# Norm outputs in chunks of 96 columns with ones behind each: column sums out of the diagonal matmuls

## The chip, the core and the metric

One core of a Trainium2 chip runs the whole program. The metric is device time in microseconds (us) of one execution. The engines are named as in the profile: PE (TensorE), DVE (VectorE), ACT (ScalarE), POOL (GpSimd) and SP (SyncE, which here only issues DMAs; POOL issues DMAs too). Every engine works through its own instructions in a fixed order and waits where an operand or a buffer is not ready.

## What is computed

A forward and backward pass of a block with two layer norms, a spectral filter and a bilinear gated unit, for 2048 rows of 576 columns (x is 1 x 2048 x 576, F is 4608). Cut to what matters here:

```
h = layernorm(x) * (1 + ca) + sa          # ca, sa, ... : rows of 576, made from c and w_mod
x1 = x + ga * spectral(h)
h2 = layernorm(x1) * (1 + cb) + sb
out = x1 + gb * ((h2 @ w_gate) * (h2 @ w_up)) @ w_down
# outputs: out and the gradients of x, both filter parts, w_gate, w_up, w_down, c and w_mod
```

The gradient of a shift (sa, sb) is the plain sum over all rows of the gradient `gh` that arrives at `h`. That of a scale (ca, cb) is the sum over rows of `gh` times the norm's output `n`, and that of `ga` the sum over rows of `gx` times `y`. These five column sums over 2048 rows (and a sixth, for gb, made elsewhere) are what the change is about.

## The kernel before, in words

The rows are held as 16 row tiles t (128 partitions, 576 columns). The program has three parts.

**Front** (about 0 to 215 us): layer norm 1, the forward spectral stages, the inverse ones, layer norm 2 (`s1_norm`, `s3_norm`), with matmuls of the backward pass dealt in as fill. The norm outputs `n1` and `n2` go to DRAM (`n1_d`, `n2_d`) and are read back in the tail, one row tile at a time (`n2c`, `n1c`).

**Body** (about 215 to 1250 us): a loop over 36 blocks of 128 of the 4608 columns, bound by PE. Its last products ("held", L793 to L799: 192 matmuls that read `h2p`, `gon` and the turned blocks `gg_sf`, `gu_sf`, L644) are not issued there but kept as fill for the tail.

**Tail** (about 1250 to 1523 us), where nearly all of the change lies:

- *Stage 1*, for each row tile t: `t1_norm` (norm 2 backward, on DVE and ACT: L873 a product with a running sum, L880 an affine step, L881 the result `gxr`, a ring of 4; POOL stores it, L989), `t1_turn` (five transposes, L998, and the sums, below), `t1_cols` and `t1_rows` (two transforms, L1017 and L1024/L1025).
- *Stage 2* (`t2_...`): 19 chunks of the spectral filter backward.
- *Stage 3*, for each row tile: `t3_rows`, `t3_cols` (L210, L212, L1209; DVE makes `ghr`, L1213 and L1214) and `t3_norm` (norm 1 backward: L1223, L873, L878 on ACT, L881; then the sums).
- The *projection* to `out` (L1286, matmuls `u3p<-wd,hl`) is fill from the end of the held products on. `hl` are blocks of the hidden activations, `wd` of w_down; a tile `u3p` takes 36 block steps fb, and in the first group two such tiles run side by side, so that fb is reached at matmul 2 x fb.
- *Sections* (L936): for each of the six rows a broadcast of the sum over partitions (`spread`, L925, an fp32 matmul against ones), ACT copies (`dmb`), five ACT and five DVE operations (L946, L952) and DMAs.

`deal` (L883) writes PE's order in the tail by hand: behind every step of stage 1 come 16 matmuls of fill (first the held ones, then the projection), behind a step of stage 2 twelve, behind a step of stage 3 sixteen. Fill that is left after stage 3 runs at the end.

**The sums before.** `diag` (L910) multiplies, for each row tile, a 128-column block of `gh` with the same 128 columns of `n`, adding up in PSUM over all t; the diagonal of each 128 x 128 result holds the wanted sums (five matmuls: four of 128 columns, one of 64). `colsum` (L907) multiplies a 0/1 matrix `pick` with both halves of `gh` (two matmuls of 288 columns). In stage 1 a step has two `colsum` and ten `diag` matmuls, in stage 3 two and five. `add_zero` (L902) opens and closes each bank with a 128 x 512 matmul of zeros. `diag_rows` (L917) takes the diagonals out on DVE, a copy (L1043, L1240) the plain sums (`dsb`, `dsa`, 128 x 288 fp32).

**Loads for the projection.** `queued_load` (L1085) ties each load to POOL's store of `gxr` number t and lets the next store follow it on POOL's queue. In POOL's order: store 2, `wd` blocks 0-6; store 3, the first `hl` (`hlt0`); store 4, `wd` 7-13; store 5, `hl` 1; store 6, `wd` 14-20; stores 7, 8, `hl` 2, `wd` 21-27; store 9, `hl` 3; store 10, `wd` 28-35 (L1091 to L1099).

**Memory.** Pools are laid one after another from the left end of each partition's memory, every tile rounded up to 32 bytes. A tile that takes over memory waits for all that still use the tiles that lay there (`reuse_waits="tile"`). Left side, in bytes per partition:

| order | body | tail |
|---|---|---|
| first | small constants with `pick` (512) | the same constants |
| then | `h2T` 20,480 | `tl0`: zeros and tables, 17,344 |
| then | `h2p` 20,480 (16 row tiles of 1,280) | `tl`: 12,928, with `sel` 1,024, `dsb` and `dsa` 1,152 each |
| then | `wT`, two of 9,216 | `o2p`: 12,672 |
| then | `hh_sf`, `gg_sf`, ... | `hlt0` 4,608 (the first `hl`), then `wd` 0-6, 7-13, ... |

Of the kernel before, what the change touches and what calls it, by code (L numbers as in the profile page):

```python
# [9 lines left out]
FP32 = mybir.dt.float32  # L10
# [9 lines left out]
NT = 16  # L20
S = 2048
D = 576
DP = 640
DF = 289
FP = 292
# [73 lines left out]
def build(ctx, tc, A_x, A_w_r, A_w_i, B_w_gate, B_w_up, B_w_down, c_in, w_mod, grad_out,  # L99
# [13 lines left out]
    def dram(name, shape, dt):  # L113
        return nc.dram_tensor(name, list(shape), dt).ap()
# [10 lines left out]
    wn_d = dram("wn_d", [128, 2 * NT * FP], BF)  # L125
    n1_d = dram("n1_d", [128, NT, D], BF)
    n2_d = dram("n2_d", [128, NT, D], BF)
    MSA, MCA, MGA, MSB, MCB, MGB = range(6)
# [12 lines left out]

    pick = glob.tile([128, 2, 128], BF, name="pick")
    nc.vector.memset(pick[:], 0.0)
    for q in range(2):
        nc.vector.memset(pick[:, q, 64 * q:64 * q + 64], 1.0)


    def traced():
# [111 lines left out]
    with ExitStack() as hs:  # L260
# [17 lines left out]
        hpp = hw2.tile([128, 3, DP], BF, name="hpp", bufs=1)  # L278
        nc.gpsimd.memset(hpp[:, :, D:DP], 0.0)
        modh = [(u4 if j == MGB else hp1).tile([128, D], BF, name="modh%d" % j) for j in range(6)]  # L280
        VA = hp1.tile([128, NG * 128], BF, name="VA")
# [77 lines left out]
        def s1_norm(t):  # L359
            c4, tt = t // 4, t % 4  # L360
            if tt == 0:
                if c4 == 1:
                    with tc.issue_after(first):
                        x_load(3)
                n1s[c4] = hw2.tile([128, 4, D], BF, name="n1")
            if t == 0 or tt == (1 if c4 == 0 else 0):
                n = 1 if t == 0 else 4 - tt
                nmr = norm_stats(xts[c4][:, tt:tt + n, :], hw2, n, "ln1", rstd1g[:, t:t + n], 4)
                for k in range(n):
                    n1s["nmr", t + k] = nmr[:, k:k + 1]  # L370
            n1 = n1s[c4]
            nc.scalar.activation(out=n1[:, tt, :], in_=xts[c4][:, tt, :], func=ACT.Identity, bias=n1s["nmr", t], scale=rstd1g[:, t:t + 1])
            nm = hw2.tile([128, D], BF, name="nm")
            nc.vector.tensor_tensor(out=nm[:], in0=n1[:, tt, :], in1=modh[MCA][:], op=MUL)
            hh = hpp[:, t % 3, :]
            nc.vector.tensor_tensor(out=hh[:, 0:D], in0=nm[:], in1=modh[MSA][:], op=ADD)
            if tt == 3:
                nc.gpsimd.dma_start(n1_d[:, t - 3:t + 1, :], n1[:])
            pt = fps.tile([128, 5, 128], BF, name="trp", tag="fp")
            for m in range(5):  # L380
                nc.tensor.transpose(pt[:, m, :], hh[:, m * 128:(m + 1) * 128], ident[:])
            hT = hTs[t] = hw2.tile([128, 5, 128], BF, name="hT")
            evac(hT[:], pt[:], eng="a")
# [148 lines left out]


        uts, ybs, h2_made = {}, {}, []

# [18 lines left out]
        def s3_norm(sa):  # L554
# [6 lines left out]
            x1 = hw2.tile([128, 2, D], BF, name="x1")  # L561
            n2 = hw2.tile([128, 2, D], BF, name="n2")
            nc.gpsimd.dma_start(y_d[:, s0:s0 + 2, :], yb[:])
# [5 lines left out]
            for i in range(2):  # L569
                nc.scalar.activation(out=n2[:, i, :], in_=x1[:, i, :], func=ACT.Identity, bias=nmr2[:, i:i + 1], scale=rstd2g[:, s0 + i:s0 + i + 1])  # L570
                nm = hw2.tile([128, D], BF, name="nm")
                nc.vector.tensor_tensor(out=nm[:], in0=n2[:, i, :], in1=modh[MCB][:], op=MUL)
                nc.vector.tensor_tensor(out=h2p[:, s0 + i, D:DP], in0=nm[:, 512:D], in1=modh[MSB][:, 512:D], op=ADD)
                h2_made.append(nc.vector.tensor_tensor(out=h2p[:, s0 + i, 0:D], in0=nm[:], in1=modh[MSB][:], op=ADD).ins)
# [236 lines left out]
    with ExitStack() as ts:  # L811
# [43 lines left out]
        dgb = tl.tile([128, D], FP32, name="dgb")[:]  # L855
        sel = tl.tile([128, 2, 128], FP32, name="sel")
        ones_b = tl.tile([128, 128], BF, name="ones_b")
# [10 lines left out]
        def norm_back(pool, gn, n, rstd, res, out, name):  # L868
# [3 lines left out]
            w = pool.tile([128, D], BF, name="w" + name, bufs=1)  # L872
            nc.vector.scalar_tensor_tensor(out=w[:], in0=gn[:], scalar=rstd, in1=n, op0=MUL, op1=MUL, accum_out=s12[:, 1:2])  # L873
            ab = pool.tile([128, 2], FP32, name="ab" + name)
            nc.vector.tensor_scalar(out=ab[:], in0=s12[:], scalar1=-1.0 / D, scalar2=None, op0=MUL)
            nc.vector.tensor_tensor(out=u[:], in0=u[:], in1=res, op=ADD)
            if name == "1":
                nc.scalar.activation(out=w[:], in_=n, func=ACT.Identity, bias=ab[:, 0:1], scale=ab[:, 1:2])  # L878
            else:
                nc.vector.tensor_scalar(out=w[:], in0=n, scalar1=ab[:, 1:2], scalar2=ab[:, 0:1], op0=MUL, op1=ADD)  # L880
            return nc.vector.tensor_tensor(out=out, in0=u[:], in1=w[:], op=ADD)  # L881
# [19 lines left out]

        def add_zero(*banks, first):  # L902

            for cs in banks:
                nc.tensor.matmul(cs[:], lhsT=ident[:], rhs=zero[:], start=first, stop=not first)

        def colsum(cs, h, src):  # L907
            nc.tensor.matmul(cs[:, 0:288], lhsT=pick[:, h, :], rhs=src, start=False, stop=False)

        def diag(cs, cs4, off, a, b):  # L910

            for m in range(5):
                o = cs[:, wide(m)] if m < 4 else cs4[:, off:off + 64]
                w = 128 if m < 4 else 64
                nc.tensor.matmul(o, lhsT=a[:, wide(m)] if m < 4 else a[:, D - 128:D], rhs=b[:, m * 128:m * 128 + w], start=False, stop=False)

        def diag_rows(pool, cs, cs4, off, name):  # L917

            d = pool.tile([128, D], FP32, name=name)
            nc.vector.tensor_tensor(out=d[:, 0:512].rearrange("p (m n) -> p m n", m=4), in0=cs[:].rearrange("p (m n) -> p m n", m=4), in1=ident[:].unsqueeze(1).to_broadcast([128, 4, 128]), op=MUL)  # L920
            nc.vector.tensor_tensor(out=d[:, 512:576], in0=cs4[:, off:off + 64], in1=ident[:, 64:128], op=MUL)
            return d
# [10 lines left out]
        def of_sums(d):  # L933
            return [lambda h=h: spread(sel[:, h, :], d[:]) for h in range(2)]

# [18 lines left out]
        with ExitStack() as r1:  # L954
# [14 lines left out]
            def t1_norm(t):  # L969
                if t == 0:  # L970
                    nc.sync.dma_start(ga_h[:], modb_d[:, MGA, :])
                for k, src, tt in [("n2c", n2_d, 0)] * (t == 0) + [("n2c", n2_d, t + 1)] * (t < NT - 1) + [("yc", y_d, t)]:
                    ld[k, tt] = c1.tile([128, D], BF, name=k, bufs=5 if k == "n2c" else 3)
                    with behind(ld["order"]):
                        ins = nc.sync.dma_start(ld[k, tt][:], src[:, tt, :])
                    ld[k, "ins", tt] = ins.ins
# [18 lines left out]
            def t1_turn(t):  # L995
# [7 lines left out]
                if t == 0:  # L1003
                    add_zero(csA, csB, csC, first=True)
                for h in range(2):
                    colsum(csB, h, gh[:, h * 288:(h + 1) * 288])
                diag(csA, csB, 288, gh, n2c)
                diag(csC, csB, 352, gx, yc)
                if t == NT - 1:
                    add_zero(csA, csB, csC, first=False)  # L1010

# [27 lines left out]
            in_order(seq)  # L1039
            dcb = diag_rows(tl, csA, csB, 288, "dcb")  # L1040
            dga = diag_rows(tl, csC, csB, 352, "dga")
            dsb = tl.tile([128, 288], FP32, name="dsb")
            nc.vector.tensor_copy(dsb[:], csB[:, 0:288])  # L1043
            with behind([i_ for i_ in nc.cur_bb.bb.instructions[-40:] if i_.engine == mybir.EngineType.DVE][-1:]):
# [57 lines left out]
        with behind([last[nc.gpsimd]]):  # L1102
            gb_h = modh(MGB, "gb_h", gbhp, nc.gpsimd)
            for q in range(2):
                nc.gpsimd.tensor_copy(sel[:, q, :], ident[:, 64 * q:64 * q + 1].to_broadcast([128, 128]))
            nc.gpsimd.memset(ones_b[:], 1.0)
            nc.gpsimd.memset(gsc[:], 0.0)
# [108 lines left out]
        def t3_norm(sa):  # L1216
            for k, src in (("n1c", n1_d), ("gxc", gx1_d)):
                ld3[k] = c3.tile([128, D], BF, name=k, bufs=5)
                nc.sync.dma_start(ld3[k][:], src[:, sa, :])
# [7 lines left out]
            if sa == 0:  # L1227
                add_zero(csD, csE, first=True)
            for h in range(2):
                colsum(csE, h, gh[:, h * 288:(h + 1) * 288])  # L1230
            diag(csD, csE, 288, gh, n1)
            if sa == NT - 1:
                add_zero(csD, csE, first=False)
            if sa in (4, 7, 10, 13):
                filter_grad(rest[sa // 3 - 1])

        pipeline(NT, [t3_rows, t3_cols, t3_norm], 3)
        dca = diag_rows(tl, csD, csE, 288, "dca")
        dsa = tl.tile([128, 288], FP32, name="dsa")
        nc.vector.tensor_copy(dsa[:], csE[:, 0:288])  # L1240
        r3.close()
# [138 lines left out]
```

## Time and profile before

| what | value |
|---|---|
| median of 3 runs (lowest, highest) | 1528.19 us (1525.73, 1534.41) |
| profiled execution | 1524.87 us, of which the span is 1523.1 us |
| PE busy, share of the span | 1490.3 us, 98% |
| DVE, ACT, POOL busy | 1060.6, 583.4, 238.8 us |
| stage 1, 2, 3, rest of the tail (read from the timeline) | 1262 to 1336, to 1392, to 1454, to 1523 us |
| DMA share and rate, 1295 to 1336 us | 0.99 of 16 engines, 311 GB/s |
| `colsum` in stage 1 and 3 (L908) | 32 + 32 matmuls, mean 286 ns each in the record |
| `diag` (L915) | 192 of 128 columns (219 ns), 48 of 64 columns (193 ns) |
| zeros (L905) | 6 of 512 columns, 379 ns |

The duration of a PE record overlaps with the next one; what a matmul costs in a stream is read from the distance between starts. "Idle before" is the time an engine stood still before a record, with the releaser that the semaphores point to.

### The profile page before, as it was taken

What the parts mean: (1) busy time and instruction counts of PE and PEld (TensorE: products, weight loads), DVE (VectorE), ACT (ScalarE), POOL (GpSimd) and SP (SyncE); (2) the same over time, 40 slices, a digit from 0 to 9 for tenths busy, and PEclk for the clock granted to TensorE, in tenths of its full rate; (3) what the DMA queues carried; (4) which work ended last, traced back from release to release, by engine and by line L of the source; (5) the groups of instructions that cost most, each with busy time, mean ns of one, the idle gap of its engine ahead of it and who ended that gap; (6) DMA issues with size and microseconds to landing.
All of it is one profiled execution on the core that took longest, in us unless ns stands there. A gap on an engine that the chain in (4) does not pass through costs nothing. (4 is left out here: it accounts for less than half of the span.)

```text
span 1523.1 us, 29031 instructions
## 1 busy us (share of the span) xinstructions
PE 1490.3 (98%) x11140; PEld 1012.6 (66%) x11144; DVE 1060.6 (70%) x2646; ACT 583.4 (38%) x1189; POOL 238.8 (16%) x363
## 2 busy tenths in 40 slices
PE   6899999999999999999999999999999999999998
PEld 4666543566666667666666676676666667888876
DVE  6866753666677767667677677676676768688884
ACT  6667742322222222222222222222222225686763
POOL 0001222101101102111111120120110113221022
PEclk9999999999999999999999999999999999999999
DMA  8968999688878768768778588688677779965587
GB/s 317 282 200 224 278 255 249 152 162 155 174 129 161 155 125 174 152 125 177 135 146 178 118 159 164 119 163 156 137 152 153 132 175 252 305 220 181 182 290 201
DMA packets 487181, 280.42 MB, mean 184 GB/s; under 512 B 408865, under 2 KB 457378, under 8 KB 486018
## 3 DMA queue, kind: packets, MB, share of 16 engines
q1 hardware_dynamic: 458882, 175.32, 55.6%
q0 software_dynamic: 28160, 103.25, 23.0%
q8 instruction: 87, 1.43, 0.4%
q14 instruction: 52, 0.43, 0.1%
HBM read 108.62 MB, written 82.31 MB: 125 GB/s over the span
## 5 line engine op out<-in xcount | busy, mean ns | idle before, releaser
L752 DVE TENSOR_TENSOR acc<-acc,u8p 128x288 f32<-128x288 f32 (+1 forms) x1088 | 483.3, 453 | 276.1 <-PE u8p L747 272.6
L747 PE MATMUL u8p<-wT,ggT 128*128 128x288 bf16 x1152 | 328.0, 286 | 1.7 <-DVE acc L752 1.6
L747 PE MATMUL u8p<-wT,guT 128*128 128x288 bf16 x1152 | 327.6, 286 | 0.0
L711 PE MATMUL gup<-h2T,wgu 128*128 128x512 bf16 x1152 | 297.8, 379 | 0.0
L646 ACT CAST so<-u57p 128x288 bf16<-128x288 f32 x216 | 86.3, 400 | 532.8 <-PE u57p L644 522.1
L644 PE MATMUL u57p<-h2p,gu_sf 128*128 128x288 bf16 x1152 | 186.4, 286 | 0.0
L644 PE MATMUL u57p<-h2p,gg_sf 128*128 128x288 bf16 x1152 | 185.9, 286 | 0.0
L711 PEld LDWEIGHTS <-wgu 128*128 128x128 bf16 x1152 | 109.6, 98 | 97.9 <-issue 17.1
L747 PEld LDWEIGHTS <-ggT 128*128 128x128 bf16 x1152 | 112.6, 98 | 66.5 <-issue 14.0
L451 PE MATMUL u4p<-goT,wdT 128*128 128x512 bf16 x656 | 151.1, 379 | 0.9 <-DVE goT L423 0.5
L747 PEld LDWEIGHTS <-guT 128*128 128x128 bf16 x1152 | 112.7, 98 | 57.6 <-issue 2.4
L1286 PE MATMUL u3p<-wd,hl 128*128 128x288 bf16 x936 | 141.3, 288 | 0.1
L713 ACT CAST gT<-gup 128x512 bf16<-128x512 f32 x144 | 84.5, 587 | 131.5 <-PE gup L711 129.6
L644 PEld LDWEIGHTS <-hh_sf 128*128 128x128 bf16 x1152 | 112.7, 98 | 28.4
L644 PEld LDWEIGHTS <-gu_sf 128*128 128x128 bf16 x1152 | 112.4, 98 | 28.5
L644 PEld LDWEIGHTS <-gg_sf 128*128 128x128 bf16 x1152 | 112.4, 98 | 28.2
L1286 PEld LDWEIGHTS <-hl 128*128 128x128 bf16 x1152 | 107.8, 98 | 25.7 <-DMA hl<-hhT_d 0.4
L713 ACT CAST uT<-gup 128x512 bf16<-128x512 f32 x144 | 84.5, 587 | 77.4 <-PE gup L711 77.4
L451 PEld LDWEIGHTS <-wdT 128*128 128x128 bf16 x656 | 61.3, 98 | 73.0 <-issue 7.6
L644 PE MATMUL u57p<-gonC,hh_sf 128*128 128x288 bf16 x576 | 99.7, 286 | 0.0
L724 POOL DMA_DIRECT2D hhT_d<-hhT x36 | 33.3, 925 | 375.5 <-DVE hhT L715 352.5
L173 DVE CAST ghh_st<-u4p 128x512 bf16<-128x512 f32 x56 | 38.7, 691 | 59.0 <-PE u4p L451 58.9
(373 smaller groups left out, 1867.6 us busy)
## 6 DMA issues: line engine op xcount, KB each, us to landing
ghhT_d<-ghh_st POOLq DMA_DIRECT2D x36, 512.0 KB, 4.3
ghh<-ghhT_d POOLq DMA_DIRECT2D x36, 512.0 KB, 7.3
hhT_d<-hhT POOLq DMA_DIRECT2D x36, 512.0 KB, 6.4
hl<-hhT_d SPq DMA_DIRECT2D x28, 576.0 KB, 6.0
out_dram<-woT SPq DMA_DIRECT2D x70, 128.0 KB, 2.0
wdn<-in_B_w_down_dram SPq DMA_DIRECT2D x18, 288.0 KB, 3.6
wd<-in_B_w_down_dram POOLq DMA_DIRECT2D x36, 144.0 KB, 4.7
out_dram<-so SPq DMA_DIRECT2D x36, 144.0 KB, 2.8
```

What stands on the lines that cost most here:

```text
L173: nc.vector.tensor_copy(dst, src)
L451: nc.tensor.matmul(pt[:], lhsT=wdTs[k][:, j, m, :], rhs=goT[:, 4 * sb4:4 * sb4 + 4, m, :], start=(m == 0 and n == 5), stop=(m == n - 1))
L644: mm = nc.tensor.matmul(pw[0][:, 0:288], lhsT=sf[:, t, :], rhs=rhs_n(t, h * 288, 288), start=(t == 0), stop=(t == NT - 1))
L646: followed(mm, nc.scalar.copy(so[:, h * 288:(h + 1) * 288], pw[0][:, 0:288]))
L711: nc.tensor.matmul(pts[k][:], lhsT=wgu[:, 4 * wi_ + m, jw * 128:(jw + 1) * 128], rhs=h2T[:, ts_, m, :], start=False, stop=(m == 3))
L713: nc.scalar.copy((gT, uT)[wi_][:, th_, :], pts[k][:])
L724: nc.gpsimd.dma_start(hhT_d[:, :, fb, :].rearrange("tp f x -> f tp x"), hhT[:].rearrange("f (tp ti) p -> f tp (ti p)", ti=2))
L747: nc.tensor.matmul(pu[:, 0:288], lhsT=l_, rhs=r_, start=(k == 0), stop=(k == len(mms) - 1))
L752: summed[t] = nc.vector.tensor_tensor(out=ghb(t)[:, hs_] if fbs[-1] == NFB - 1 else dst, in0=dst, in1=pu[:, 0:288], op=ADD).ins
L1286: mm = nc.tensor.matmul(p2[ti][:, 0:288], lhsT=hls[fb // 9][:, fb % 9, ti * 128:(ti + 1) * 128], rhs=w[:, fb - f0, h * 288:(h + 1) * 288], ...
```

## The change

Norm outputs are stored as six chunks of 96 columns, each followed by two columns of ones (row of 588 instead of 576). A `diag` matmul then takes 96 columns of `n` and one column of ones: the diagonal still gives the scale's sum, the 97th column the plain sum over rows. So `colsum`, `pick` and `sel` go, `diag` has six matmuls of 97 (96 for `ga`) columns in place of five, and the closing zeros go (the last `diag` matmuls close the banks). The plain sums come out as `[128, 6]`; where they are used, `of_sums` spreads each of the six columns over a masked identity (three DVE operations per half) ahead of the fp32 matmul. Operations that read or write `n1`, `n2` do so in six pieces of 96 (`part`). The ones are written once by POOL into two fixed buffers per norm.

```diff
+DC = 96
+DS = 98
+DN = 6 * DS
...
-    n1_d = dram("n1_d", [128, NT, D], BF)
-    n2_d = dram("n2_d", [128, NT, D], BF)
+    n1_d = dram("n1_d", [128, NT, DN], BF)
+    n2_d = dram("n2_d", [128, NT, DN], BF)
-    pick = glob.tile([128, 2, 128], BF, name="pick")
-    nc.vector.memset(pick[:], 0.0)
-    for q in range(2):
-        nc.vector.memset(pick[:, q, 64 * q:64 * q + 64], 1.0)
-
+    def part(ap):
+        return ap.rearrange("p (m c) -> p m c", m=6)[:, :, 0:DC]
+    def ones_between(ap):
+        nc.gpsimd.memset(ap.rearrange("p t (m c) -> p (t m) c", c=DS)[:, :, DC:DS], 1.0)
...
+        n1r = [hw2.tile([128, 4, DN], BF, name="n1r%d" % k, bufs=1) for k in range(2)]
+        for n_ in n1r:
+            ones_between(n_[:])
...
-            nc.scalar.activation(out=n1[:, tt, :], in_=xts[c4][:, tt, :], func=ACT.Identity, bias=n1s["nmr", t], scale=rstd1g[:, t:t + 1])
+            nc.scalar.activation(out=part(n1[:, tt, :]), in_=part(xts[c4][:, tt, :]), func=ACT.Identity, bias=n1s["nmr", t], scale=rstd1g[:, t:t + 1])
...
-        sel = tl.tile([128, 2, 128], FP32, name="sel")
...
-            nc.vector.scalar_tensor_tensor(out=w[:], in0=gn[:], scalar=rstd, in1=n, op0=MUL, op1=MUL, accum_out=s12[:, 1:2])
+            nc.vector.scalar_tensor_tensor(out=part(w[:]), in0=part(gn[:]), scalar=rstd, in1=part(n), op0=MUL, op1=MUL, accum_out=s12[:, 1:2])
...
-                nc.scalar.activation(out=w[:], in_=n, func=ACT.Identity, bias=ab[:, 0:1], scale=ab[:, 1:2])
+                nc.scalar.activation(out=part(w[:]), in_=part(n), func=ACT.Identity, bias=ab[:, 0:1], scale=ab[:, 1:2])
             else:
-                nc.vector.tensor_scalar(out=w[:], in0=n, scalar1=ab[:, 1:2], scalar2=ab[:, 0:1], op0=MUL, op1=ADD)
+                nc.vector.tensor_scalar(out=part(w[:]), in0=part(n), scalar1=ab[:, 1:2], scalar2=ab[:, 0:1], op0=MUL, op1=ADD)
...
-        def colsum(cs, h, src):
-            nc.tensor.matmul(cs[:, 0:288], lhsT=pick[:, h, :], rhs=src, start=False, stop=False)
...
+        def diag(cs, cs6, off, a, b, step, w, last_, shut=True):
+            for m in range(6):
+                o = cs[:, m * w:m * w + w] if m < 5 else cs6[:, off:off + w]
+                c0 = m * DC if m < 5 else D - 128
+                nc.tensor.matmul(o, lhsT=a[:, c0:c0 + 128], rhs=b[:, m * step:m * step + w], start=False, stop=last_ and m >= 4 and (m == 4 or shut))
...
+        def diag_sums(pool, cs, cs6, off, name):
+            d = pool.tile([128, 6], FP32, name=name)
+            for m0, m1, _, src in chunks(cs, cs6, off, DC + 1):
+                nc.vector.tensor_copy(d[:, m0:m1].unsqueeze(2), src[:, :, DC:DC + 1])
+            return d
...
         def of_sums(d):
-            return [lambda h=h: spread(sel[:, h, :], d[:]) for h in range(2)]
+            def half(h):
+                x = secp.tile([128, 288], FP32, name="dx", bufs=1)
+                for m in range(3 * h, 3 * h + 3):
+                    mask = ident[:, 0:DC] if m < 5 else ident[:, 128 - DC:128]
+                    nc.vector.tensor_scalar(out=x[:, m % 3 * DC:m % 3 * DC + DC], in0=mask, scalar1=d[:, m:m + 1], scalar2=None, op0=MUL)
+                return spread(ones_f[:], x[:])
+            return [lambda h=h: half(h) for h in range(2)]
...
-                    add_zero(csA, csB, csC, first=True)
-                for h in range(2):
-                    colsum(csB, h, gh[:, h * 288:(h + 1) * 288])
-                diag(csA, csB, 288, gh, n2c)
-                diag(csC, csB, 352, gx, yc)
-                if t == NT - 1:
-                    add_zero(csA, csB, csC, first=False)
+                    add_zero(csA, csB, csC)
+                diag(csA, csB, 0, gh, n2c, DS, DC + 1, t == NT - 1, False)
+                diag(csC, csB, 128, gx, yc, DC, DC, t == NT - 1)
...
-            dsb = tl.tile([128, 288], FP32, name="dsb")
-            nc.vector.tensor_copy(dsb[:], csB[:, 0:288])
+            dsb = diag_sums(tl, csA, csB, 0, "dsb")
```

Stage 3 is changed in the same way (`csD`, `csE`, `dsa`), the front's `n2` like `n1`, and the two POOL copies that made `sel` go. `deal` and the pools' order are not touched.

More of the change, by code (lines that the diff above doesn't have):

```diff
@@ L364, in s1_norm @@
                         x_load(3)
-                n1s[c4] = hw2.tile([128, 4, D], BF, name="n1")
+                n1s[c4] = n1r[c4 % 2]
             if t == 0 or tt == (1 if c4 == 0 else 0):
@@ L371, in s1_norm @@
             n1 = n1s[c4]
-            nc.scalar.activation(out=n1[:, tt, :], in_=xts[c4][:, tt, :], func=ACT.Identity, bias=n1s["nmr", t], scale=rstd1g[:, t:t + 1])
+            nc.scalar.activation(out=part(n1[:, tt, :]), in_=part(xts[c4][:, tt, :]), func=ACT.Identity, bias=n1s["nmr", t], scale=rstd1g[:, t:t + 1])
             nm = hw2.tile([128, D], BF, name="nm")
-            nc.vector.tensor_tensor(out=nm[:], in0=n1[:, tt, :], in1=modh[MCA][:], op=MUL)
+            nc.vector.tensor_tensor(out=part(nm[:]), in0=part(n1[:, tt, :]), in1=part(modh[MCA][:]), op=MUL)
             hh = hpp[:, t % 3, :]
@@ L531, in build @@
         hw2 = pool("hc3", 2, "right")
+        n2r = [hw2.tile([128, 2, DN], BF, name="n2r%d" % k, bufs=1) for k in range(2)]
+        for n_ in n2r:
+            ones_between(n_[:])
         uts, ybs, h2_made = {}, {}, []
@@ L561, in s3_norm @@
             x1 = hw2.tile([128, 2, D], BF, name="x1")
-            n2 = hw2.tile([128, 2, D], BF, name="n2")
+            n2 = n2r[sa // 2 % 2]
             nc.gpsimd.dma_start(y_d[:, s0:s0 + 2, :], yb[:])
@@ L569, in s3_norm @@
             for i in range(2):
-                nc.scalar.activation(out=n2[:, i, :], in_=x1[:, i, :], func=ACT.Identity, bias=nmr2[:, i:i + 1], scale=rstd2g[:, s0 + i:s0 + i + 1])
+                nc.scalar.activation(out=part(n2[:, i, :]), in_=part(x1[:, i, :]), func=ACT.Identity, bias=nmr2[:, i:i + 1], scale=rstd2g[:, s0 + i:s0 + i + 1])
                 nm = hw2.tile([128, D], BF, name="nm")
-                nc.vector.tensor_tensor(out=nm[:], in0=n2[:, i, :], in1=modh[MCB][:], op=MUL)
+                nc.vector.tensor_tensor(out=part(nm[:]), in0=part(n2[:, i, :]), in1=part(modh[MCB][:]), op=MUL)
                 nc.vector.tensor_tensor(out=h2p[:, s0 + i, D:DP], in0=nm[:, 512:D], in1=modh[MSB][:, 512:D], op=ADD)
@@ L900, in wide, with add_zero @@
             return slice(m * 128, (m + 1) * 128)
-        def add_zero(*banks, first):
+        def add_zero(*banks):
             for cs in banks:
-                nc.tensor.matmul(cs[:], lhsT=ident[:], rhs=zero[:], start=first, stop=not first)
-        def colsum(cs, h, src):
[L908 to L915, printed above, removed]
@@ L917, in diag_rows @@
-        def diag_rows(pool, cs, cs4, off, name):
-            d = pool.tile([128, D], FP32, name=name)
-            nc.vector.tensor_tensor(out=d[:, 0:512].rearrange("p (m n) -> p m n", m=4), in0=cs[:].rearrange("p (m n) -> p m n", m=4), in1=ident[:].unsqueeze(1).to_broadcast([128, 4, 128]), op=MUL)
-            nc.vector.tensor_tensor(out=d[:, 512:576], in0=cs4[:, off:off + 64], in1=ident[:, 64:128], op=MUL)
+                nc.tensor.matmul(cs[:], lhsT=ident[:], rhs=zero[:], start=True, stop=False)
@@ new lines, in diag, with chunks @@
+        def diag(cs, cs6, off, a, b, step, w, last_, shut=True):
[3 more added lines that the diff above has]
+                nc.tensor.matmul(o, lhsT=a[:, c0:c0 + 128], rhs=b[:, m * step:m * step + w], start=False, stop=last_ and m >= 4 and (m == 4 or shut))
+        def chunks(cs, cs6, off, w):
+            for m0, m1, mask, src in ((0, 5, ident[:, 0:DC], cs[:, 0:5 * w]), (5, 6, ident[:, 128 - DC:128], cs6[:, off:off + w])):
+                yield m0, m1, mask.unsqueeze(1).to_broadcast([128, m1 - m0, DC]), src.rearrange("p (m c) -> p m c", c=w)
@@ new lines, in diag_rows @@
+        def diag_rows(pool, cs, cs6, off, w, name):
+            d = pool.tile([128, D], FP32, name=name)
+            for m0, m1, mask, src in chunks(cs, cs6, off, w):
+                nc.vector.tensor_tensor(out=d[:, m0 * DC:m1 * DC].rearrange("p (m n) -> p m n", n=DC), in0=src[:, :, 0:DC], in1=mask, op=MUL)
+            return d
[3 more added lines that the diff above has]
+                nc.vector.tensor_copy(d[:, m0:m1].unsqueeze(2), src[:, :, DC:DC + 1])
@@ L972, in t1_norm @@
                 for k, src, tt in [("n2c", n2_d, 0)] * (t == 0) + [("n2c", n2_d, t + 1)] * (t < NT - 1) + [("yc", y_d, t)]:
-                    ld[k, tt] = c1.tile([128, D], BF, name=k, bufs=5 if k == "n2c" else 3)
+                    ld[k, tt] = c1.tile([128, DN if k == "n2c" else D], BF, name=k, bufs=5 if k == "n2c" else 3)
                     with behind(ld["order"]):
@@ L1039, in build @@
             in_order(seq)
-            dcb = diag_rows(tl, csA, csB, 288, "dcb")
-            dga = diag_rows(tl, csC, csB, 352, "dga")
-            dsb = tl.tile([128, 288], FP32, name="dsb")
-            nc.vector.tensor_copy(dsb[:], csB[:, 0:288])
+            dcb = diag_rows(tl, csA, csB, 0, DC + 1, "dcb")
+            dga = diag_rows(tl, csC, csB, 128, DC, "dga")
+            dsb = diag_sums(tl, csA, csB, 0, "dsb")
             with behind([i_ for i_ in nc.cur_bb.bb.instructions[-40:] if i_.engine == mybir.EngineType.DVE][-1:]):
@@ L1103, in build @@
             gb_h = modh(MGB, "gb_h", gbhp, nc.gpsimd)
-            for q in range(2):
-                nc.gpsimd.tensor_copy(sel[:, q, :], ident[:, 64 * q:64 * q + 1].to_broadcast([128, 128]))
             nc.gpsimd.memset(ones_b[:], 1.0)
@@ L1217, in t3_norm @@
             for k, src in (("n1c", n1_d), ("gxc", gx1_d)):
-                ld3[k] = c3.tile([128, D], BF, name=k, bufs=5)
+                ld3[k] = c3.tile([128, DN if k == "n1c" else D], BF, name=k, bufs=5)
                 nc.sync.dma_start(ld3[k][:], src[:, sa, :])
@@ L1227, in t3_norm @@
             if sa == 0:
[L1228 to L1233, printed above, removed]
+                add_zero(csD, csE)
+            diag(csD, csE, 0, gh, n1, DS, DC + 1, sa == NT - 1)
             if sa in (4, 7, 10, 13):
@@ L1237, in build @@
         pipeline(NT, [t3_rows, t3_cols, t3_norm], 3)
-        dca = diag_rows(tl, csD, csE, 288, "dca")
-        dsa = tl.tile([128, 288], FP32, name="dsa")
-        nc.vector.tensor_copy(dsa[:], csE[:, 0:288])
+        dca = diag_rows(tl, csD, csE, 0, DC + 1, "dca")
+        dsa = diag_sums(tl, csD, csE, 0, "dsa")
         r3.close()
```

## The prediction

> **What bounds the kernel now.** I read the page first:
>
> ```profile
> span 1523.1 us, 29031 instructions
> ...
> PE 1490.3 (98%) x11140; PEld 1012.6 (66%) x11144; DVE 1060.6 (70%) x2646; ACT 583.4 (38%) x1189; POOL 238.8 (16%) x363
> ```
>
> PE never rests, so a column taken from PE is worth its time where PE is what is late, and a wait put on PE costs its whole length. Then I read the timelines of the tail, PE's first, one step of stage 1 (start, duration, engine, line; the distance of two starts is what a record costs):
>
> ```profile
> 1302.47 0.44 PE L998 MATMUL trp<-ident,gxf 128*128 128x128 bf16 x5
> 1302.75 0.41 PE L908 MATMUL csB<-acc,pick 128*128 128x288 bf16 x2
> 1302.99 0.39 PE L915 MATMUL csA<-n2c,acc 128*128 128x128 bf16 x4
> 1303.22 0.19 PE L915 MATMUL csB<-n2c,acc 128*128 128x64 bf16 x1
> 1303.24 0.39 PE L915 MATMUL csC<-yc,gxr 128*128 128x128 bf16 x4
> 1303.47 0.19 PE L915 MATMUL csB<-yc,gxr 128*128 128x64 bf16 x1
> 1303.50 1.14 PE L1286 MATMUL u3p<-wd,hl 128*128 128x288 bf16 x8
> 1304.48 0.29 PE L1024 MATMUL vp<-zt,T_G 128*128 128x292 bf16 x1
> ```
>
> The sums take 1302.75 to 1303.50, 0.75 us: two of 288 columns 0.24, four of 128 columns 0.23, one of 64 some 0.025. All go by columns, 0.425 ns each (eight of 288: 0.98 us).
>
> In stage 3 the records that count are DVE's:
>
> ```profile
> 1408.55 0.46 DVE L881 TENSOR_TENSOR ob<-u,w 128x576 bf16<-128x576 bf16 x1 [0.58 <-ACT w L878]
> ...
> 1410.27 0.82 DVE L873 SCALAR_TENSOR_TENSOR w<-gn,rstd1g,n1c 128x576 bf16<-128x576 bf16 x1
> ...
> 1412.31 0.46 DVE L881 TENSOR_TENSOR ob<-u,w 128x576 bf16<-128x576 bf16 x1 [0.58 <-ACT w L878]
> ```
>
> The period is 3.76 us, of which DVE stands still only for ACT's `w` (0.58); no PE result is ever late there.
>
> **Term 1, PE's columns.** A stage 1 step streams 2 x 288 + 2 x 576 = 1728 columns for its sums; after the change 6 x 97 + 6 x 96 = 1158. 570 x 0.425 ns = 0.24 us per step. In steps 1 to 7 (period 4.58 us) the sums lie on the loop from PE's `zp` over ACT's `b_Vp` back to PE, in steps 8 to 15 PE itself is the bound; step 0 waits for `gxf` and gains nothing: 15 x 0.24 = **-3.6**. The closing zeros go: three in stage 1 at 0.21 (start to start 1329.40 to 1329.61), two after stage 3: **-1.1**. Bounds: columns at 0.425 ns; or no piece below what one of 128 costs, 12 x 0.0555 = 0.67 per step, which leaves 0.08 (-1.2 in place of -3.6). The row of 64 columns (0.025) speaks for the first. Together **-4.7**.
>
> A row's rule beside this: the Trainium skill ("TensorE: Matmul & The Clock Gate", "Back-to-back issue gap") gives a sustained stream of weight-load and matmul pairs about 81 ns per matmul at 128 columns, and says the column formula under-counts small ones; by it twelve matmuls would be an estimated 0.97 us per step and the change would lose there. This trace's pairs of 128 columns stand 55 to 58 ns apart, so it does not agree.
>
> **Term 2, stage 3: nothing.** 0.49 us of sums becomes 0.25, 16 x 0.24 = 3.8 us of PE's work, but DVE and ACT set the 3.76 us (above) and fill is dealt out by count. PE would wait for `ghr` by what it saves. Bounds: 0 to -3.8; I take 0, since the 0.58 wait for ACT stands in every step.
>
> **DVE and ACT in pieces of 96.** Pieces cost about nothing in the nearest rows: a DVE product in runs of 16 takes 420 ns for 512 columns, plain ones 455 for 576; an ACT copy in four runs 405 against 407. L880, if it fell to L873's rate (0.82 in place of 0.43), would add 0.39 to DVE's 3.7 in a step of 4.3, which still fits. Rows of 1176 bytes in place of 1152 add 2% to 32 loads. The ones (some 0.14 us per memset) lie on POOL before `n1` is first written, and in a 4.4 us pause before `n2`. The two POOL copies of `sel` and DVE's copies of 288 become copies of six numbers, off every path. All **0**; what hides them is DVE's slack, 0.6 us a step.
>
> **Term 3, the memory of the first `hl`.** This is the large one. By the memory table the tail's `tl` loses `sel` 1,024 and 2 x (1,152 - 32): 3,264 bytes. `hlt0` started at 17,344 + 12,928 + 12,672 = 42,944, beyond `h2p`, whose end is 40,960; it will start at 39,680, 1,280 bytes inside it: its last row tile (`pick`'s 512 shift both alike). A tile that takes over memory waits for all readers of the old tile, and the last reader of `h2p` is the last held matmul:
>
> ```profile
> 1294.68 1.14 PE L644 MATMUL u57p<-h2p,gu_sf 128*128 128x288 bf16 x8
> ```
>
> Before, the first `hl` waits for nothing; the fourth one, whose memory held `gu_sf`, does what the first will do (POOL):
>
> ```profile
> 1268.45 0.54 POOL L1064 DMA_DIRECT2D hl<-hhT_d  x1
> ...
> 1271.67 0.55 POOL L989 DMA_DIRECT2D gx_d<-gxr  x1 [2.68 <-DVE gxr L881]
> ...
> 1296.12 0.54 POOL L1064 DMA_DIRECT2D hl<-hhT_d  x1 [0.98 <-PE vp L1025]
> ```
>
> So the first `hl` moves from 1268.45 to the end of the held matmuls, 1295.66 - 7 x 0.24 = 1294.0. Queued behind it on POOL: stores 4 to 10, the later `wd` and `hl`, 7.5 MB with it (4 x 0.576, 3 x 1.008, 1.152, 7 x 0.144), now issued within some 9 us at 0.54 to 0.99 us each. No deadlock: the held matmuls need only `gxr` 7, the ring holds 4 and store 3 is ahead. At 311 GB/s (window 1295 to 1336)
>
> ```profile
> 1295.00:1336.00 41.00, 40.79 (x397) 33.23 (x397) 24.50 (x72) 25.18 (x63) 11.93 (x24) 1.00 0.99 311
> ```
>
> and 411 in the best 15 us of it, 7.5 MB plus some 2 MB of SP's loads last 18 to 30 us, and `wd` 28-35 lands at 1315 to 1326. PE needs it at projection matmul 56, three and a half steps of 4.0 us after 1294.5: 1308.5. Lateness 6.5 to 17.5; earlier blocks are less late: `hl` itself some 4 us, by the tile's view of its four loads,
>
> ```profile
> DMA to landing us min/median/max: 3.9/6.5/9.5
> ```
>
> PE has no other fill then, so the wait is lost. The rate next to it in time is 311, at a share of 0.99 already: I take **+13**.
>
> **Term 4, sections.** `of_sums` now puts three DVE operations of 0.2 to 0.3 us before each half, six per section, in two sections, into one `x` whose second half waits for PE's first. PE already waits there:
>
> ```profile
> 1475.64 1.19 PE L927 MATMUL spp<-dgb,ones_f 128*128 128x288 f32 x2 [2.40 <-ACT dmb L939]
> ```
>
> since ACT waits for DVE's products of the section before. Lower bound 0 (fill follows and covers it), upper bound 12 x 0.3 and the hand-overs, some 6; the section for sb, which ran inside stage 3, may take DVE time there. I take **+2**.
>
> **Sum.** -4.7 + 0 + 13 + 2 = +10.3. Against the profiled execution's 1524.87 this is 1535.2; the median of the runs shown lies 3.3 above that execution, and on it 1528.2 + 10.3 = **1538.5**.
>
> **The rivals.**
> - *The queue drains quickly.* The first `hl` is late, but what follows runs at 411 GB/s and the last block is 6.5 us late: -4.7 + 6.5 + 2 = +3.8, 1532. For it: the best 15 us. Against: most stretches run at 263 to 311.
> - *The other side: the first `hl` does not wait*, since its tile is laid elsewhere or the held readers are gone sooner. Then -4.7 + 2 = -2.7: 1525.5, not slower. It decides at 1294.5: if `hl` and `wd` 0-6 are there by then, nothing is lost; every us later costs one. Against it: the bytes of the table and the fourth `hl`.
> - *A floor per pair*: pieces of 96 go at the 0.0555 us of the 128-wide rows: +2.4 on the forecast, 1541. Against it the 64-wide row's 0.025. (The Trainium skill's section named above sets the floor higher: at its 81 ns the forecast would rise by an estimated 7.)
> - *Stage 3 is PE's after all*: 3.8 us more saved, +6.5, 1534.7. Against it the 0.58 us for ACT in each step.
>
> That the sums don't come out of the diagonals can't be: the matmuls that made them are gone.
>
> **How the numbers follow.** Forecast 0.58 (own range 1535 to 1547), quick queue 0.21, no wait 0.09, pace of 128 0.05, stage 3 0.07. A measurement of this kernel can tell 0.5%, 7.6 us, from no change: 1520.6 to 1535.8. Faster takes the no-wait case with stage 3's gain on top (-6.5) and more: 0.04. Same: quick queue, stage 3, most of no wait, and the forecast's low edge: 0.35. Slower: 0.61. The range leaves out the no-wait case and reaches to the quick queue (less 4, where sections cost nothing and stage 3 gains a little) and up to lateness 17.5 with sections at +6 (+18.8): 1528 to 1547.
>
> **What would show it.** Right: the first `hl` on POOL issued at 1294 behind an idle of some 25 us that ends by PE; PE idle at L1286 for DMA of `hl` and `wd` between 1294 and 1326, some 13 us in sum; 0.50 us of sums per step of stage 1; a period of 3.76 in stage 3 with PE waiting for `ghr`; idle time of PE before `spp`. Wrong: the first `hl` at 1268; stage 3 at 3.5 us per step; sums of 0.67 us or more.

## The result and the profile after

Over nine runs the changed kernel takes 1540.26 us at the median (1534.41 to 1548.70), the kernel before 1529.27 (1524.98 to 1536.59) over nine; the ratio is 1.0065, with a 95% interval of 1.0040 to 1.0089: 10 us more, between 6 and 14. The profiled execution took 1540.26 us. The page says:

```profile
span 1538.5 us, 29000 instructions
...
PE 1488.8 (97%) x11123; PEld 1006.7 (65%) x11123; DVE 1059.9 (69%) x2657; ACT 582.0 (38%) x1189; POOL 238.0 (15%) x365
```

PE has 1.5 us less work and 15.4 us more span: PE waits. Where, is read by laying the two timelines of PE side by side and taking, for the same matmul, the start after less the start before:

| matmul | before | after | lag |
|---|---|---|---|
| a late one of the front's inverse spectral stage | 190.64 | 195.61 | +5.0 |
| a held one in the middle of stage 1 | 1285.52 | 1288.86 | +3.3 |
| the first of the projection (`hl`) | 1296.16 | 1303.49 | +7.3 |
| a transform of stage 1, 18 us on | 1314.32 | 1334.41 | +20.1 |
| the first behind stage 1's sums | 1329.83 | 1348.54 | +18.7 |
| a late one of stage 3 | 1451.59 | 1468.74 | +17.2 |
| end of the span | 1523.1 | 1538.5 | +15.4 |

So 16.8 us come in one place, from 1285.52 to 1314.32 of before (3.3 to 20.1), 5.0 in the front, and 6.4 are won back elsewhere (1.7 before the first projection matmul, 1.4, 1.5 and 1.8 behind it). Most of the 1.5 is only moved: four matmuls of a section (`spp`), which ran inside stage 3 before (1450.32 to 1451.59), come behind it now.

**The large place.** POOL's timeline of the changed kernel (start, duration, then idle before and what ended it):

```profile
1272.55 0.58 POOL L1015 DMA_DIRECT2D gx_d<-gxr  x1 [1.61 <-DVE gxr L891]
1299.05 0.54 POOL L1085 DMA_DIRECT2D hl<-hhT_d  x1 [25.93 <-PE vp L1047]
1299.58 0.55 POOL L1015 DMA_DIRECT2D gx_d<-gxr  x1
...
1320.79 0.54 POOL L1085 DMA_DIRECT2D hl<-hhT_d  x1
```

The first `hl` stands 25.93 us on POOL, until just behind the last held matmul (`vp`, which the view names, is the second matmul after it), and with it all that is queued behind; the fourth one, at 1296.12 before, is issued at 1320.79. PE's waits from 1250 to 1345 us (in total, times, longest), in the same kernel:

```profile
PE u3p L1300 <- DMA hl<-hhT_d: 6.0, 2, 4.2
PE u3p L1300 <- DMA wd<-in_B_w_down_dram: 5.5, 3, 2.8
```

Before, PE had no wait for either:

```profile
PE u8p L747 <- DVE acc L752: 1.3, 1, 1.3
PE zp L1017 <- ACT b_Vp L1026: 1.2, 7, 0.2
```

6.0 + 5.5 = 11.5 us are standing still; the other 5 are a slower PE, which the table by stretches shows in its third column from the right, the granted clock:

```profile
1299.00:1303.40 4.40, 0.25 (x2) 0.00 (x0) 0.00 (x0) 0.18 (x1) 2.05 (x3) 1.00 0.89 232
1303.40:1307.00 3.60, 2.62 (x13) 1.59 (x14) 2.97 (x10) 2.08 (x6) 2.24 (x5) 0.59 0.94 315
1307.00:1311.00 4.00, 4.00 (x30) 3.09 (x29) 2.69 (x10) 1.65 (x4) 3.56 (x5) 0.52 0.94 259
1311.00:1315.00 4.00, 3.54 (x40) 2.76 (x38) 3.16 (x11) 2.81 (x7) 0.00 (x0) 1.00 1.00 351
...
1327.00:1331.00 4.00, 1.23 (x8) 0.71 (x5) 2.61 (x8) 1.13 (x3) 0.00 (x0) 0.62 0.87 306
1331.00:1336.00 5.00, 5.00 (x33) 3.44 (x32) 0.44 (x2) 2.04 (x6) 0.00 (x0) 0.62 0.01 2
```

After 4.2 us without matmuls PE works for some 7 us at about half its clock: from 1307 to 1311 it counts as fully busy and gets 30 matmuls done, then 40 in 3.54 us. (The Trainium skill, "TensorE: Matmul & The Clock Gate", "Part 1: The HAM clock gate", says that the clock halves after an idle window of about 3.4 us and comes back after as long a busy one. The rows agree with the half, and the return took about two such windows. The trace does not agree with the idle window each time: from 1327 to 1336 the granted clock was down again, at 0.62, with the last wait for `wd`, which took 2.8 us.)

**Stage 1's sums** in the changed kernel, undisturbed:

```profile
1339.74 0.39 PE L922 MATMUL csA<-n2c,acc 128*128 128x97 bf16 x5
1339.97 0.21 PE L922 MATMUL csB<-n2c,acc 128*128 128x97 bf16 x1
1340.02 0.38 PE L922 MATMUL csC<-yc,gxr 128*128 128x96 bf16 x5
1340.23 0.21 PE L922 MATMUL csB<-yc,gxr 128*128 128x96 bf16 x1
1340.27 1.14 PE L1300 MATMUL u3p<-wd,hl 128*128 128x288 bf16 x8
```

1339.74 to 1340.27 is 0.53 us where it was 0.75: twelve matmuls, 44 ns each.

**Stage 3** keeps its period; DVE and then PE of the changed kernel:

```profile
1427.11 0.46 DVE L891 TENSOR_TENSOR ob<-u,w 128x576 bf16<-128x576 bf16 x1 [0.58 <-ACT w L888]
...
1430.87 0.46 DVE L891 TENSOR_TENSOR ob<-u,w 128x576 bf16<-128x576 bf16 x1 [0.58 <-ACT w L888]
```

```profile
1426.77 0.60 PE L215 MATMUL upa<-T_GB,j_A 128*128 128x256 bf16 x4
1427.42 0.27 PE L217 MATMUL upb<-T_GB,j_At 128*128 128x128 bf16 x2
```

1427.11 to 1430.87 is 3.76 us, to the hundredth what it was, and the time saved on the sums is a gap in PE: `upb` starts 0.65 us after `upa`, where before it was 0.45:

```profile
1412.17 0.60 PE L210 MATMUL upa<-T_GB,j_A 128*128 128x256 bf16 x4
1412.62 0.27 PE L212 MATMUL upb<-T_GB,j_At 128*128 128x128 bf16 x2
```

**The front.** What DVE waits for between 100 and 215 us in the changed kernel:

```profile
DVE x L577 <- DMA xc<-in_A_x_dram: 11.6, 5, 3.8
```

Before it was less:

```profile
DVE x L566 <- DMA xc<-in_A_x_dram: 5.0, 4, 2.5
```

Whether the change did that had to be tried.

### The profile page after: what moved, and what is told of

Its sections match the earlier page's. It is cut to its first block, busy times and chain, and to the rows that moved or that the text cites. A ratio compares the mean times of both kernels' runs of the same rounds, so it can differ in the third digit from the quotient of the medians.

```text
span 1538.5 us, 29000 instructions
## 1 busy us (share of the span) xinstructions
PE 1488.8 (97%) x11123; PEld 1006.7 (65%) x11123; DVE 1059.9 (69%) x2657; ACT 582.0 (38%) x1189; POOL 238.0 (15%) x365
## 4 chain that ended last, share of the span: by engine, by line
PE 81%; DVE 7%; DMA 6%; issue 3%; ACT 2%; POOL 1%; SPq 0%; POOLq 0%; DVEq 0%; ACTq 0%
PE u57p L655 27%; PE u8p L758 18%; PE gup L722 16%; PE u4p L459 7%; PE u3p L1300 4%; PE gup L717 3%; DMA xc<-in_A_x_dram 2%; DMA wmj<-in_w_mod_dram 1%; DVE ln_st L186 1%; PE zp L398 1%; ACT w L888 1%; DVE w L883 1%; PE u4p L454 1%; DVE goT L430 1%; DMA wd<-in_B_w_down_dram 1%
```

## The experiments

The theory (A): the loss is the memory hand-over, 1,280 bytes of `h2p` under the first `hl`, by way of the loads queued behind it on POOL; what is left of the change is a small gain. Its rivals: (B) the change is dear elsewhere, in the front above all; (C) the pieces of 96 columns are dear; and, within A, that the `hl` itself costs it all, not the queue.

### The overlap taken away: e1_clear

```diff
         gsc = tl.tile([128, 5, 6], FP32, name="gsc")
+        tl.tile([128, 640], BF, name="pad")
```

> The changed kernel with an unused tile of 1,280 bytes at the end of the tail's table pool, so that the first hl block starts exactly at the end of h2p; nothing else differs. Theory A (the memory hand-over is the loss): the first hl is issued on POOL right behind the store of gxr number 3 instead of 26 us later, PE has no wait for hl or wd between 1295 and 1330 us (12.1 us in the changed kernel) and the granted clock there is 1.00 again instead of 0.83 (some 4.6 us more), so 16.7 us go: about 1523 us, ratio to before 0.996 (0.993 to 1.000). Rival B (the change costs elsewhere: the front, where DVE waited 11.6 us for loads of x in the changed kernel's trace and 5.0 in that of before, is 6.8 us longer by the change): ratio 1.000 to 1.004. Rival C (the pieces of 96, not the memory): ratio stays at 1.0065.

Measured: 1527.97 us (12 runs) beside 1531.85 of before (27 runs), ratio 0.998 (0.9957 to 1.0002). POOL and PE's waits from 1250 to 1345 us:

```profile
1272.07 0.58 POOL L1016 DMA_DIRECT2D gx_d<-gxr  x1 [1.61 <-DVE gxr L892]
1272.65 0.54 POOL L1086 DMA_DIRECT2D hl<-hhT_d  x1
```

```profile
PE csC L923 <- DMA yc<-y_d: 3.9, 1, 3.9
```

The `hl` goes out right behind the store, and the waits for `hl` and `wd` are gone; C falls, since all pieces of 96 are still there. The one wait for a DMA that is there, for `yc`, was not expected (see the runs made again). The front's wait for `xc` was 9.8 us in this trace.

### 32 bytes of it left: e2_32bytes

```diff
         gsc = tl.tile([128, 5, 6], FP32, name="gsc")
+        tl.tile([128, 624], BF, name="pad")
```

> The changed kernel with an unused tile of 1,248 bytes instead of 1,280: the first hl block lies 32 bytes inside h2p. Theory A (a tile that takes over memory waits for every reader of the old tile, however little of it is taken): the whole loss is back, POOL idle some 26 us before the first hl, ratio to before 1.0065 (1.004 to 1.009), some 16 us above the kernel with 1,280 bytes. Rival (the wait is for what was in the overlapped bytes, or the loss has to do with where the tables lie): near the kernel with 1,280 bytes.

Measured: 1542.65 us (10 runs), ratio 1.0077 (1.0049 to 1.0105). POOL:

```profile
1267.88 0.58 POOL L1016 DMA_DIRECT2D gx_d<-gxr  x1 [1.61 <-DVE gxr L892]
1294.39 0.54 POOL L1086 DMA_DIRECT2D hl<-hhT_d  x1 [25.93 <-PE vp L1048]
```

32 bytes more or less decide over 14.7 us (1542.65 less 1527.97, on one chip); nothing else in the text of the two kernels differs. A stands: the overlap is the cause. It does more than A says, though: POOL's written order is another one too (see the part on the prediction). This trace's front is as quick as that of before (`xc` 5.6 us in three waits), though the front is the changed one.

### The overlap alone, in the kernel before: e3_overlap

```diff
-        sel = tl.tile([128, 2, 128], FP32, name="sel")
+        sel = mvp.tile([128, 2, 128], FP32, name="sel")
...
-            dsb = tl.tile([128, 288], FP32, name="dsb")
+            dsb = mvp.tile([128, 288], FP32, name="dsb")
...
-        dsa = tl.tile([128, 288], FP32, name="dsa")
+        dsa = mvp.tile([128, 288], FP32, name="dsa")
```

`mvp` is a new pool behind the `wd` blocks; sums and norms are those of before. The three tiles have 1,024 + 2 x 1,152 = 3,328 bytes, so the first `hl` lies 1,344 bytes inside `h2p` here, 64 more than the expectation says.

> The kernel before, sums and norms untouched, with sel, dsb and dsa (3,264 bytes) moved from the table pool to one behind the wd blocks, so that the first hl block starts 1,280 bytes inside h2p. Theory A: the loss alone, without the change: the first hl waits until about 1296 us, PE waits some 12 us for hl and wd and runs at a lower granted clock behind it, ratio 1.011 (1.007 to 1.014). Rival B or C: 1.000.

Measured: 1553.32 us (6 runs), ratio 1.0142 (1.0098 to 1.0186). POOL:

```profile
1303.98 0.54 POOL L1065 DMA_DIRECT2D hl<-hhT_d  x1 [27.67 <-PE vp L1026]
```

A change that computes nothing new loses 22 us (15 to 28), just above the range that was expected. That is more than the 14.7 above; part of it is that here the held matmuls end later (the `hl` waits 27.67 and not 25.93 us) and PE's waits for `hl` and `wd` sum up to 13.7; for the rest the intervals are wide. And this trace has the longest of the front's waits, with the front of before:

```profile
DVE x L566 <- DMA xc<-in_A_x_dram: 13.7, 5, 3.9
```

Waits for `xc` of 5.0, 13.7 and 12.5 (below) with the old front, and between 4.1 and 11.6 with the new one: they come and go from run to run, whatever the front. The start of the tail follows them: DVE's first `gxr` comes at 1249.8, 1257.7 and 1258.0 us with the old front, and between 1247.4 (wait of 4.1) and 1255.2 (8.8) with the new one. B falls for the front; the 5 us there belong to the two traces, not to the change.

### The load moved back on its queue: e4_hl_later

```diff
-        first_hl = [queued_load(3, hl_load, 0, nc.gpsimd)]
+        first_hl = []
...
+        first_hl.insert(0, queued_load(9, hl_load, 0, nc.gpsimd))
         first_hl.append(queued_load(9, hl_load, 3, nc.gpsimd))
```

Each load keeps its own tile.

> The changed kernel, memory as in it, but the first hl moved on POOL's queue from behind the store of gxr number 3 to behind number 9, just ahead of the fourth hl: it waits for the held matmuls as before, but stores 4 to 9 and the wd blocks 7 to 27 go ahead of it and no longer wait with it. Theory (most of the loss is what is queued behind the waiting load, not the load): PE waits for the first hl alone, 4 to 6.5 us by the landing times, plus 1 to 3 us of lower clock: 5 to 9 us above the changed kernel with 1,280 unused bytes, ratio to before 1.001 to 1.004. Rival (the hl itself costs all of it): ratio 1.0065 to 1.0077, as the changed kernel and the one with 1,248 bytes.

Measured: 1530.52 us (12 runs), ratio 1.0021 (1.0001 to 1.0041). By the ratios that is 6 us above e1_clear and 8 to 9 below e2_32bytes (of 1530 us, 0.0041 and 0.0056). PE:

```profile
1304.05 1.14 PE L1301 MATMUL u3p<-wd,hl 128*128 128x288 bf16 x4 [7.64 <-DMA hl<-hhT_d]
```

One wait of 7.6 us, longer than I gave it, and none for `wd`. So the `hl` itself does not cost all of it, and what stands behind it in the queue costs something too. Which part is the larger these runs don't tell, since either difference is uncertain by 4 to 5 us; and in this kernel POOL's stores stand in the order of before, so that the second part holds the other order as well.

### The free time of stage 3 used: e5_more_fill and e6_before_fill

```diff
-                q = 16 if stage == 1 else 12 if stage == 2 else 20 if k == 0 else 16
+                q = 16 if stage == 1 else 12 if stage == 2 else 20 if k == 0 else 18
```

In the first with the tile of 1,280 bytes, in the second in the kernel before.

> The changed kernel with the 1,280 bytes and 18 instead of 16 fill matmuls behind each step of stage 3 (the first keeps 20). If DVE and ACT set stage 3's period of 3.76 us and PE has 0.24 us free per step since the change, two more fill matmuls (0.245 us) per step go in at no cost and 15 x 0.245 = 3.7 us less fill is left at the end: 3 to 4 us below the kernel with 1,280 bytes and 16, and the period stays at 3.76. If PE set the period: no difference, and a period of 3.9 or more.

> The kernel before with 18 instead of 16 fill matmuls behind each step of stage 3. If PE had no free time there before the change (it needed 3.74 of 3.76 us per step), the period rises to about 3.99, stage 3 takes 3.5 us more and the rest 3.7 us less: ratio 1.000 (0.998 to 1.002), so that the gain of the changed kernel with 18 is owed to the columns saved. Rival (the fill was dealt too thin before, and the change has no part in that gain): ratio 0.9975.

Measured: e5_more_fill 1524.25 us (12 runs), ratio 0.9956 (0.9929 to 0.9983), 3.7 us below e1_clear beside it, which is about as much as the uncertainty of that difference; e6_before_fill 1527.77 us, ratio 0.9991 (0.9971 to 1.0011). The periods of stage 3, by DVE, first e5_more_fill, then e6_before_fill:

```profile
1426.86 0.46 DVE L892 TENSOR_TENSOR ob<-u,w 128x576 bf16<-128x576 bf16 x1 [0.57 <-ACT w L889]
1430.62 0.46 DVE L892 TENSOR_TENSOR ob<-u,w 128x576 bf16<-128x576 bf16 x1 [0.58 <-ACT w L889]
```

```profile
1429.03 0.46 DVE L881 TENSOR_TENSOR ob<-u,w 128x576 bf16<-128x576 bf16 x1 [0.58 <-ACT w L878]
1433.03 0.46 DVE L881 TENSOR_TENSOR ob<-u,w 128x576 bf16<-128x576 bf16 x1 [0.57 <-ACT w L878]
```

3.76 with the saved columns, 4.00 without. So the change does make 0.24 us per step free in stage 3, and nothing in the program took it up; two more fill matmuls do. It is the periods that show this: the interval of e6_before_fill holds the 1.000 that was expected and the 0.9975 of the rival.

### The old layout, and runs made again: e7, e8, e9, e10

The tile of unused bytes at 3,264 (`[128, 1632]`), which puts all behind it back to where it was: e7_old_layout_fill with 18 fill matmuls, e8_old_layout with 16. e9 and e10 are e1 and e5 once more, on the same chip as e8.

> The changed kernel with 3,264 unused bytes in the table pool, so that all that lies behind it starts where it started before the change, and 18 fill matmuls per step of stage 3. If only the 1,280 bytes of overlap mattered: as the kernel with 1,280 bytes and 18, ratio 0.9956 (0.993 to 0.998). Rival (the wd blocks behind the first hl also came to lie on something that is released late, which is why PE still had 1 to 4 us of waits for yc and wd between 1300 and 1316 us there): those waits go, ratio 0.993 to 0.9945, and the projection's loads are issued earlier.

> The changed kernel with 3,264 unused bytes, so that all behind the table pool starts where it did before the change; 16 fill matmuls as in the changed kernel. If only the overlap with h2p mattered, it takes the same time as the kernel with 1,280 bytes, run beside it again (within 2 us; ratio 0.998). If the wd blocks' place matters too, it is 2 to 4 us below that one (ratio 0.995 to 0.9965), and PE has no wait for yc or wd between 1295 and 1320 us where the other has some us.

> The changed kernel with 1,280 unused bytes once more, beside the one with 3,264: ratio 0.998 (0.9957 to 1.0002) as in its first run. If PE's wait of 3.9 us for yc there came from the layout, it is in this trace again at about the same place; if it was chance among the DMAs, it is elsewhere or gone.

> The changed kernel with 1,280 unused bytes and 18 fill matmuls once more: 3.7 us below the one with 16 beside it (ratio 0.9956 in its first run), and a wait of PE for yc or wd in stage 1 if the layout makes one.

| kernel | unused bytes | fill | median us (runs) | ratio to before | PE's waits for `yc`, `wd`, 1250 to 1345 |
|---|---|---|---|---|---|
| e1_clear | 1,280 | 16 | 1527.97 (12) | 0.9980 (0.9957 to 1.0002) | 3.9 |
| e9_clear_again | 1,280 | 16 | 1519.57 (7) | 0.9954 (0.9931 to 0.9978) | 1.4 |
| e8_old_layout | 3,264 | 16 | 1523.88 (9) | 0.9971 (0.9950 to 0.9991) | 2.5 |
| e5_more_fill | 1,280 | 18 | 1524.25 (12) | 0.9956 (0.9929 to 0.9983) | 1.8 |
| e10_more_fill_again | 1,280 | 18 | 1519.72 (6) | 0.9937 (0.9915 to 0.9960) | 3.2 |
| e7_old_layout_fill | 3,264 | 18 | 1518.88 (7) | 0.9939 (0.9912 to 0.9967) | 0 |

The layout beyond the 1,280 bytes makes no difference that these runs tell: 0.9971 lies between the two runs of the smaller tile, and the waits are there with either. So the rival of e7 and e8 is not borne out, though e7 alone had seemed to bear it out. The time that the fill gains is not well known: by the ratios it is 0.0024 (e1 to e5), 0.0017 (e9 to e10) and 0.0032 (e8 to e7), 3 to 5 us and each near its uncertainty, and the medians of e9 and e10 do not differ at all. The changed kernel without its overlap and with 18 fill matmuls takes 0.4 to 0.6% less than the kernel before in all three of its runs.

## Why the prediction was right

The time came out 1.8 us from the number (1540.3 for 1538.5), the difference about as forecast (11.0 between the medians, 10 by the ratio, for 10.3). That it came so close is partly luck: term 3 was 2 to 4 us too small, term 4 some 3 too large (+2, where the waits fell by 1.2), and the two offset each other. By its steps:

- **Term 3, the memory of the first `hl`** (+13). The mechanism is shown: 32 bytes switch it on and off, and it acts alone in the kernel before. The size: 14.7 us between e2_32bytes and e1_clear, 16.8 in the one trace. Two of its parts were off. *What I left out:* the clock. I had counted a late block as time lost once, but after a 4 us wait PE runs at half clock, which made some 5 us in this trace; no term of the prediction has it. *What I had wrong:* the queue. I let POOL issue everything within 9 us and the DMAs' rate set the end. In the trace POOL stops again, for 9.70 us ahead of the store at 1320.26, waiting for DVE's `gxr` (POOL, then the `gxr` that ends the wait):

```profile
1309.01 0.98 POOL L1085 DMA_DIRECT2D wd<-in_B_w_down_dram  x1
1309.97 0.58 POOL L1015 DMA_DIRECT2D gx_d<-gxr  x1
1320.26 0.55 POOL L1015 DMA_DIRECT2D gx_d<-gxr  x1 [9.70 <-DVE gxr L891]
...
1322.09 0.90 POOL L1085 DMA_DIRECT2D wd<-in_B_w_down_dram  x1 [0.23 <-DMA out_dram<-wo_l]
```

```profile
1319.50 0.45 DVE L891 TENSOR_TENSOR gxr<-u,w 128x576 bf16<-128x576 bf16 x1
```

  Counted on DVE's timeline this is the `gxr` of row tile 12; that of tile 9 was done at 1309.02. So the store that waits is number 12, and it stands ahead of the fourth `hl`, where before only store 9 stood between `wd` 21-27 and that `hl`:

```profile
1291.05 0.98 POOL L1064 DMA_DIRECT2D wd<-in_B_w_down_dram  x1
1294.56 0.59 POOL L989 DMA_DIRECT2D gx_d<-gxr  x1 [2.53 <-DVE gxr L881]
```

  POOL's written order is thus not the one I had counted with. Laid out instruction by instruction, the programs of the three kernels with the overlap at the old place of the load (the changed one, e2_32bytes, e3_overlap) have store 8 ahead of store 5, and store 12 ahead of the fourth `hl` and store 10; those of the kernel before, e1_clear, e4_hl_later and e8_old_layout do not. Why the layout changes the order the runs don't show. The overlap brings the wait and this order together, and no run has the first `hl` wait at that place without the other order. A second link is in the trace too: DVE had waited 10.0 us for the stores of `gxr` held up behind the first `hl` (a ring of 4; 7.9 us of it ahead of 1303.99), so that store 12 and the loads behind it were later still. No run takes these two apart either. The DMAs did not set the end: from 1295 to 1336 their share was 0.85 and their rate 253 GB/s, below the 0.99 and 311 of before. The last wait for `wd` ended at 1329.87, which less the 4.7 us of the front (1272.55 for 1267.87) is 1325: inside my 1315 to 1326, by another road.
- **Term 1, PE's columns** (-4.7). Right: 0.53 us per step for 0.50, and the lag falls from 4.25 (matmul at 1266.83 of before) to 3.34 (at 1285.52), 0.9 in four steps. Twelve matmuls at 44 ns lie near the price by columns (41) and far from the 55 of the rival. The Trainium skill ("TensorE: Matmul & The Clock Gate", "Back-to-back issue gap") has some 81 ns for 128 columns in a sustained stream; this trace does not agree. The three kernels without the overlap and with 16 fill matmuls give 0.9954 to 0.9980, -3 to -7 us, for term 1 and term 4 together; I had -2.7.
- **Term 2, stage 3** (0). Right: the period did not move, and e5 and e6 show that the gain was there and lay idle. Wrong is where PE waits: not for `ghr` at the sums (but for the last step, 0.7 us), but ahead of `upb`, 0.2 us in a step, where the longer of these waits are put down to ACT's `ye`.
- **DVE and ACT in pieces** (0). Right: L883 takes 818 ns for 819, L890 426 for 425, ACT's `n2` pair 1.62 us for 1.63.
- **Term 4, sections** (+2). This step failed, in its sign. PE's waits for the sections behind stage 3 were 2.4 us before, all for `dmb`; in the changed kernel they are

```profile
PE spp L946 <- DVE dx L957: 0.7, 2, 0.5
...
PE spp L946 <- ACT dmb L965: 0.5, 1, 0.5
```

  The wait for the new `dx` is there, but smaller than the wait it does away with: the section for sb now comes behind stage 3 and not inside it, and the ones after it no longer crowd on `dmb`. Kernels with the old sums wait 1.6 to 2.4 us there, those with the new ones and 16 fill matmuls 1.0 to 1.5. That the new order of the sections is the cause is read from the timelines, not tried.

Of the rivals, "the quick queue" (1532) fell with POOL's second stop, "no wait" was wrong in the kernel as it is and is e1_clear once the overlap is gone, "a floor per pair" and "stage 3 is PE's" are answered by 44 ns and 3.76 us.

What stays open: how much of the loss is the first `hl`'s wait and how much POOL's other order, why e3_overlap lost more than e2_32bytes against e1_clear, and why PE sometimes waits 1 to 4 us for `yc` or `wd` once the sums are short (none in the traces of before and of e6_before_fill, some in five of six of the new ones). PE reaches them some 2 us sooner there, and the DMAs' share from 1295 to 1336 is 0.98 to 1.04 in these five traces, but no run tells these apart.

## What to carry to other kernels

A tile that shrinks moves all that is laid behind it: after a change of any size, lay out the memory again and look for a tile that now touches one that is released late, be it by 32 bytes. Read the written order of the queues again as well: it can change with the layout, as POOL's did here. A load that waits on a queue also delays what stands behind it (here 8 to 9 us beside the 6 of the load itself, both uncertain); and where that queue carries the stores which the loop needs, the loads behind it may become later still, which was read from a trace here and not tried. A gain on an engine that does not set the period stays idle until work is moved there: count the fill again.

## What the runs showed of the hardware

PE's clock: after waits of 4.2 and 7.6 us the granted clock was 0.5 to 0.6 for the next 4 to 8 us, so that the waits of the changed kernel cost about 1.5 times their length in its trace (16.8 for 11.5). Short matmuls: with a weight load each, pieces of 96 and 97 columns stood 44 ns apart. The front's loads of x: DVE's wait for them lay between 4.1 and 13.7 us in twelve traces of nearly the same front, whichever of the two it was, and the start of the tail lay 10.5 us apart in them (first `gxr` at 1247.4 to 1258.0). The runs of one kernel differ by 8 to 16 us (before: 1524.98 to 1536.59); how much of that arises in the front was not measured.
